# Time mixing in a fused RWKV-6 and expert kernel: the POOL marker gone, queries on DVE, gate results in spare columns of the score banks, the gate over two steps

## The chip, the cores and the metric

The kernel runs on one core of a Trainium2 chip. The metric is the device time of one execution in microseconds (us). A core has a matrix engine (PE, with weight loads shown apart as PEld), a vector engine (DVE), an activation engine (ACT), a general engine (POOL), and SP, which here only issues DMAs. Each engine works through its own queue in order; they meet through semaphores. SBUF is the on-chip memory, PSUM the banks that PE writes.

## What is computed

Two stages. Time mixing (RWKV-6) over 4 batches, 8 heads, 768 positions and head size 48, with a state per head that decays by `w` at each position:

```python
for t in range(S):
    cur = np.einsum('bhd,bhe->bhde', u[None] * kt, vt)
    y[:, :, t] = np.einsum('bhd,bhde->bhe', rt, state + cur)
    state = wt[:, :, :, None] * state + np.einsum('bhd,bhe->bhde', kt, vt)
```

Its result, as 3072 tokens of width 384, goes to a gate of two levels (the best of 4 groups, then the best of that group's 4 experts, each with its softmax weight), and to the one expert chosen: `out = weight * (relu(x @ w1[g, e]) @ w2[g, e])`, with an inner width of 1024.

## The kernel before

**Steps.** Time mixing is cut into 16 steps, `n` = 0 to 15: four batches of `HP` = 4 pairs of heads. One of the pair lies on partitions 0 to 63 and one on 64 to 127. In a step the 768 positions are 12 chunks of 64. The loop `for n in range(TOTAL + 1)` is a software pipeline written by hand for PE, DVE and ACT (`manual_schedule`): their instructions run in the order of the code. POOL and SP are ordered by the planner of the language.

**One step in the order of its code.** `masked(n)`: PE makes two tiles of scores (L311), `q` by `kk` and `ru` by `rk`; DVE masks the first (L318, `at`) and copies the diagonal from the second (L321). `growth(n)`: PE multiplies keys and values (L342), ACT copies the result to `g` (L347). For step n+1, `scaled` makes `ru` and `tot` on ACT (L279, L281), `prefixes` makes the running products `e` on DVE (L287, L289, and the scan L291), `queries` makes `q` = r times e on POOL (L296). `outer(n-1)`: PE adds the contribution of the states to `y` (L387), ACT copies `y` to `xt` (L395). `keys(n+1)` transposes `kk` on PE (L329) with a copy on ACT (L336). `states(n)` is a scan on DVE (L352, `ze`). `suffixes(n+2)` is the scan `s` on DVE (L267) and `kk` = k times s on POOL (L272). `inner(n)`: PE adds the masked scores times the values to `y` (L368), of which there is one buffer. Then loads, `finish(n-1)` and `ordered(n)` (ACT, L362, `zs`).

**The marker.** In `outer`, the half with `cross` set writes to the PSUM bank that matmuls of `inner` of the same step write from other rows of the array. It waits for `mark`, a one-element memset on POOL (L373) that waits for the matmuls of `inner`.

**Gate.** `finish` transposes `xt` into rows of tokens `x` (PE L329, ACT L403) and computes logits on PE (L413) in two banks of their own: 72 matmuls for three pairs of heads when the third of a batch is done, 24 for the last. `gate` runs once a batch, at n = 6, 10, 14 and 16: 19 small DVE operations in a row (L109 to L441), with an exponential on ACT and, in the middle, two matmuls (L428, L429) that count the tokens ahead of each token. Its result `dest` is the slot of every token. `put` sends rows of 128 tokens there with indirect DMAs issued by POOL (L448), six a batch.

**Loads.** SP issues the loads of `w` and `rk` (L159, L164); ACT's queue issues `v` (L168), the weights of the first two experts (L94, L95, at n = 5) and `blanks`, which writes empty slots to the scratch memory (L257, four a step at n = 0 to 3).

**Experts.** After the last `put` the rows are loaded again by expert (`xg`), transposed, multiplied with both weights (L592, L624, L636, L638) and scattered to the output by POOL (L614). The change leaves this part alone.

Of the kernel before, what the change touches and what calls it, by code (L numbers as in the profile page):

```python
# [31 lines left out]
I32 = mybir.dt.int32  # L33
# [15 lines left out]
def rwkv_then_moe(  # L49
# [48 lines left out]
    def choose(pool, lg, n):  # L98
# [14 lines left out]
        nc.scalar.activation(out=low, in_=low, func=AF.Exp)  # L113
# [13 lines left out]
    def weigh(pool, gone, low, sums, n, weight):  # L127
        nc.vector.tensor_reduce(out=sums, in_=low, axis=AX.X, op=ALU.add)
# [10 lines left out]
    with ExitStack() as first:  # L139
# [27 lines left out]
        def load_values(b):  # L167
            nc.scalar.dma_start(out=vts[b % 2][:, 0:VL], in_=v_d[b])  # L168


        nc.vector.memset(ws[0], 1.0)
        nc.gpsimd.memset(rks[0], 0.0)
        load_decays(0)
        load_pair(0)
        first_of = ip.tile([128, WP], F32, name="first_of", tag="first_of")
        nc.vector.memset(first_of, 0.0)
        nc.vector.memset(first_of[:, 0:WP:C + 1], 1.0)
# [4 lines left out]
        gs = [ip.tile([128, D, NB], F32, name=f"g{i}", tag=f"g{i}") for i in range(2)]  # L182
        u_sb = const([128, HP], F32, "u_sb")
        nc.vector.memset(u_sb, 0.0)
        for t in range(2):
            nc.scalar.dma_start(out=u_sb[64 * t:64 * t + D, :], in_=u_d[t])
        for i in range(2):
            nc.vector.memset(ss[i][:, WP:WP + 1], 1.0)
            nc.vector.memset(tots[i][:, :, 0:1], 0.0)
            nc.vector.memset(ivs[i], 0.0)  # L190
        nc.vector.memset(ws[1], 1.0)
        nc.gpsimd.memset(rks[1], 0.0)
        load_decays(1)
# [15 lines left out]
        nc.vector.tensor_scalar(out=si, in0=si, scalar1=C - 1, scalar2=None, op0=ALU.bitwise_and)  # L209
        diag_mask = const([128, C], U8, "diag_mask")  # L210
        nc.vector.tensor_tensor(out=diag_mask, in0=ti, in1=si, op=ALU.is_equal)
        later = const([128, C], F32, "later")
        nc.vector.tensor_tensor(out=later, in0=ti, in1=si, op=ALU.is_gt)

        def numbers(shape, pattern, base, name, mult=0):
            i = const(shape, I32, name + "_i")
            nc.gpsimd.iota(i, pattern=pattern, base=base, channel_multiplier=mult)
            f = const(shape, F32, name)
            nc.vector.tensor_copy(out=f, in_=i)
            return f  # L220
# [10 lines left out]
        wr = const([128, HP, NL], F32, "wr")  # L231
        nc.vector.memset(wr, 0.0)


        seen = const([128, NE], F32, "seen")
        nc.vector.tensor_copy(out=seen, in_=base_of)
        within = const([128, NE, NCH], F32, "within")
        nc.vector.memset(within, 1.0)
        nc.vector.memset(within[:, :, 0:1], 0.0)

        nc.gpsimd.memset(rks[2], 0.0)
        load_pair(2)
        nc.gpsimd.memset(ws[3], 1.0)
        load_decays(3)
        for t in range(2):
            nc.sync.dma_start(
                out=wr[64 * t:64 * t + D],
                in_=wr_d.rearrange("(h t d) n -> t d h n", h=HP, t=2)[t])
        for i in range(2):
            nc.gpsimd.memset(gs[i][:, :, 0:1], 0.0)  # L250
            nc.gpsimd.memset(vts[i][:, VL:], 0.0)
        blank = ip.tile([CAP // 2, 2, RW], F32, name="blank", tag="blank")
        nc.gpsimd.memset(blank, 0.0)
        nc.gpsimd.memset(blank[:, :, DM:DM + 1].bitcast(I32), N)
# [622 lines left out]
```

## Time and profile before

| | us |
|---|---|
| median of 3 runs (lowest to highest) | 580.56 (579.84 to 583.07) |
| the profiled execution | 582.13 |
| its span, first to last instruction | 580.3 |
| time mixing, first scores (step 0) to the first put of the last batch | 15.13 to 243.81 |
| experts, to the end of the span | 257.50 to 580.30 |

A row of the timeline reads: start, duration, engine, line, operation, output <- inputs, shape, count, and in brackets how long the engine had been idle and what released it. "issue" is idle time for which the profile shows no wait. The first scores of step n (L311) stand at 15.13 us (step 0), 24.38 (1), 40.43 (2), 48.52 (3), 65.58 (4), 75.99 (5), 86.26 (6), 100.23 (7), 121.87 (8), 131.83 (9), 142.22 (10), 156.80 (11), 177.12 (12), 187.50 (13), 195.75 (14) and 207.37 (15).

### The profile page before, as it was taken

What the parts mean: (1) busy time and instruction counts of PE and PEld (TensorE: products, weight loads), DVE (VectorE), ACT (ScalarE), POOL (GpSimd) and SP (SyncE); (2) the same over time, 40 slices, a digit from 0 to 9 for tenths busy, and PEclk for the clock granted to TensorE, in tenths of its full rate; (3) what the DMA queues carried; (4) which work ended last, traced back from release to release, by engine and by line L of the source; (5) the groups of instructions that cost most, each with busy time, mean ns of one, the idle gap of its engine ahead of it and who ended that gap; (6) DMA issues with size and microseconds to landing.
All of it is one profiled execution on the core that took longest, in us unless ns stands there. A gap on an engine that the chain in (4) does not pass through costs nothing. (4 is left out here: it accounts for less than half of the span.)

```text
span 580.3 us, 16365 instructions
## 1 busy us (share of the span) xinstructions
PE 468.0 (81%) x7346; PEld 406.9 (70%) x7346; DVE 230.3 (40%) x337; ACT 156.2 (27%) x345; POOL 127.5 (22%) x131
## 2 busy tenths in 40 slices
PE   0656966787477758339999999998999999999990
PEld 0645855587456647338988899888888988898880
DVE  7949389548946941301142455241011101110100
ACT  2445354245435612101211121112111211121110
POOL 7423143523363440120111001010100110001100
PEclk9889698678859955559999999999999999999996
DMA  8997479734242023043555867765646564555000
GB/s 206 252 254 218 138 233 314 263 82 132 60 124 45 5 76 92 14 140 108 190 219 177 259 213 254 231 233 210 243 155 230 172 234 163 215 185 208 16 14 21
DMA packets 20974, 95.77 MB, mean 165 GB/s; under 512 B 4038, under 2 KB 7627, under 8 KB 16288
## 3 DMA queue, kind: packets, MB, share of 16 engines
q1 hardware_dynamic: 14240, 68.63, 38.5%
q10 hardware_dynamic: 3328, 16.55, 8.8%
q0 software_dynamic: 3328, 9.47, 4.4%
q8 instruction: 59, 0.97, 0.7%
q14 instruction: 19, 0.16, 0.1%
HBM read 79.64 MB, written 15.78 MB: 164 GB/s over the span
## 5 line engine op out<-in xcount | busy, mean ns | idle before, releaser
L592 PE MATMUL bank_a<-xt,w 128*128 128x224 f32 x768 | 150.9, 357 | 0.6 <-DVE xt L606 0.6
L592 PEld LDWEIGHTS bank_a<-xt,w 128*128 128x128 f32 x768 | 145.1, 191 | 3.4 <-issue 2.3
L614 POOL DMA_INDIRECT out_dram<-yo,xg x32 | 30.9, 964 | 288.0 <-DVE yo L619 233.2
L624 PE MATMUL bank_b<-w,ht 128*128 128x384 f32 x256 | 85.6, 488 | 0.0
L594 ACT ACTIVATE ht<-bank_a 128x224 f32<-128x224 f32 x128 | 45.7, 357 | 111.4 <-PE bank_a L592 110.0
L619 DVE TENSOR_SCALAR yo<-bank_b,xg 128x384 f32<-128x384 f32 (+1 forms) x32 | 18.1, 566 | 136.7 <-PE bank_b L624 80.6
L624 PEld LDWEIGHTS bank_b<-w,ht 128*128 128x128 f32 x256 | 47.5, 190 | 29.7
L636 PE MATMUL bank_b<-w,ht 128*32 128x288 f32 x768 | 66.8, 409 | 0.0
L638 PE MATMUL bank_b<-w,ht 128*32 128x96 f32 x768 | 66.4, 246 | 0.0
L638 PEld LDWEIGHTS bank_b<-w,ht 128*32 128x32 f32 x768 | 62.9, 110 | 0.0
L606 DVE COPY xt<-bank_b 128x384 f32<-128x384 f32 (+1 forms) x32 | 14.8, 503 | 105.5 <-PE bank_b L604 105.5
L645 ACT COPY yo<-bank_b 32x96 f32<-32x96 f32 x48 | 11.1, 232 | 161.1 <-DVE yo L619 160.8
L636 PEld LDWEIGHTS bank_b<-w,ht 128*32 128x32 f32 x768 | 46.9, 108 | 8.7 <-issue 7.6
L296 POOL TENSOR_TENSOR q<-rk,e 128x768 f32<-128x768 f32 x16 | 37.0, 2312 | 73.1 <-DVE e L291 30.9
L387 PE MATMUL y<-q,zs 64*48 64x64 f32 x704 | 32.5, 251 | 17.7 <-issue 15.7
L267 DVE TENSOR_TENSOR_SCAN s<-w,first_of 128x780 f32<-128x780 f32 x16 | 42.6, 2662 | 1.4 <-DMA w<-in_w_dram 1.4
L387 PEld LDWEIGHTS y<-q,zs 64*48 64x48 f32 x704 | 28.5, 145 | 20.7 <-issue 18.2
L342 PE MATMUL bank<-v,kt 64*64 64x48 f32 x704 | 24.3, 242 | 14.3 <-issue 13.9
L272 POOL TENSOR_TENSOR kk<-rk,s 128x768 f32<-128x768 f32 x16 | 27.3, 1704 | 32.6 <-DVE s L267 14.9
L448 POOL DMA_INDIRECT slot_scratch<-x,dest x24 | 24.4, 1018 | 42.1 <-DVE dest L441 26.0
L342 PEld LDWEIGHTS bank<-v,kt 64*64 64x64 f32 x704 | 20.4, 156 | 16.7 <-issue 16.7
L347 ACT COPY g<-bank 128x288 f32<-128x288 f32 (+1 forms) x32 | 11.6, 420 | 69.0 <-PE bank L342 44.1
(132 smaller groups left out, 516.1 us busy)
## 6 DMA issues: line engine op xcount, KB each, us to landing
w<-in_w_dram SPq DMA_DIRECT2D x28, 1536.0 KB, 6.5
rk<-in_rk_dram SPq DMA_DIRECT2D x32, 288.0 KB, 9.4
w<-in_w_dram ACTq DMA_DIRECT2D x4, 1536.0 KB
slot_scratch<-blank ACTq DMA_DIRECT2D x16, 337.8 KB, 5.8
w<-in_w_dram SPq DMA_DIRECT2D x32, 146.2 KB, 5.5
wt<-in_w_dram SPq DMA_DIRECT2D x4, 1170.0 KB
v<-in_v_dram ACTq DMA_DIRECT2D x4, 1152.0 KB
xg<-slot_scratch SPq DMA_DIRECT2D x16, 193.0 KB
```

Source lines behind the costliest of these rows:

```text
L267: nc.vector.tensor_tensor_scan(out=p["s"][:, 0:WP][:, ::-1], data0=p["w"][:, ::-1], data1=first_of[:, ::-1], initial=1.0, op0=ALU.mult, op ...
L272: nc.gpsimd.tensor_tensor(out=blocked(kk), in0=blocked(p["rk"][:, 1]), op=ALU.mult, in1=p["s"][:, 1:].rearrange("p (n c) -> p n c", c=C + ...
L296: nc.gpsimd.tensor_tensor(out=blocked(p["q"]), in0=blocked(p["rk"][:, 0]), op=ALU.mult, in1=p["e"].rearrange("p (n c) -> p n c", c=C + 1)[ ...
L342: nc.tensor.matmul(zs[j][halves[t], c * D:(c + 1) * D], lhsT=p["kt"][halves[j], c, halves[t]], rhs=value(p, c, t, D)[halves[j]], start=Tru ...
L387: m = nc.tensor.matmul(p["y"][j][64 * t:64 * t + D, C * c:C * (c + 1)], lhsT=p["zs"][halves[t], i], rhs=p["q"][halves[t], C * i:C * (i + 1 ...
L448: m = nc.gpsimd.indirect_dma_start(out=slot_dram, out_offset=bass.IndirectOffsetOnAxis(ap=dest[:, c:c + 1], axis=0), in_=x[:, c, :], in_of ...
L592: nc.tensor.matmul(z[:, 0:n], lhsT=w1[:, dc, f * 128:(f + 1) * 128], rhs=xt[:, dc], start=(dc == 0), stop=(dc == DC - 1))
L594: nc.scalar.activation(out=ht[:, f], in_=z[:, 0:n], func=AF.Relu)
L614: nc.gpsimd.indirect_dma_start(out=out, out_offset=bass.IndirectOffsetOnAxis(ap=to, axis=0), in_=yo[0:m], in_offset=None, bounds_check=N - ...
L624: nc.tensor.matmul(z[0:m, 0:DM], lhsT=ht[:, f, 0:m], rhs=w2[:, f], start=(f == 0), stop=(f == FC - 1))
L636: nc.tensor.matmul(z[32 * g:32 * (g + 1), 0:q], lhsT=lhs, rhs=w2[:, f, 0:q], start=(f == 0), stop=(f == FC - 1), skip_group_check=True)
L638: nc.tensor.matmul(z[96:128, 96 * g:96 * (g + 1)], lhsT=lhs, rhs=w2[:, f, q:], start=(f == 0 and g == 0), stop=(f == FC - 1), skip_group_c ...
```

## The change

- The marker goes. The `cross` half of `outer(n)`, which runs in step n+1, now waits for an instruction that is there anyway and follows `inner(n)`: the last ACT copy of `rows(n-1)` (L418), or, for step 0, the mask multiplication of step 1 (`behind_inner`).
- `queries` moves from POOL to DVE (L305); `q` has three buffers instead of two. POOL keeps `kk` (L279) and the puts.
- Logits and the gate's counts are written to the columns of the second score tile that the scores leave free, instead of banks of their own. So they stand on PE right behind the scores, ahead of `growth`. Logits are split two pairs and two pairs (in the last batch three and one), and their sums over both halves are one DVE reduction (L435).
- The gate is a generator that is resumed at three places: choice and scan after `states` of one step, the two matmuls after the scores of the next, the rest after `queries` of that step. The exponential moves to the start of the last part. Three puts are issued after `kk` of a later step, and three a step later.
- SP joins the hand-written order. All loads, the values and the blanks too, go through SP's queue; blanks at n = 1 to 4, from a tile of half the size that is read twice; weights of expert 0 at n = 5, of expert 1 at n = 7.
- `growth` stands after `ru`, `tot` after `keys`, `rows` right after `inner`; `xt` has three buffers. In the setup, conversions move from DVE to ACT, and part of it behind the first `kk`.

```diff
         def load_values(b):
-            nc.scalar.dma_start(out=vts[b % 2][:, 0:VL], in_=v_d[b])
...
+            nc.sync.dma_start(out=vts[b % 2][:, 0:VL], in_=v_d[b])
+
+        first.enter_context(tc.manual_schedule(engines={
+            ENG.PE, ENG.DVE, ENG.Activation, ENG.SP}))
...
         def queries(p):
-            p["q"] = p2.tile([128, S], F32, name="q", tag="q")
-            nc.gpsimd.tensor_tensor(
+            p["q"] = p2.tile([128, S], F32, name="q", tag="q", bufs=3)
+            nc.vector.tensor_tensor(
...
-            p["behind"] = nc.gpsimd.memset(mark, 0.0)
-            for m in ms:
-                tc.add_manual_dep(p["behind"].ins, m.ins.name, AFTER,
-                                  reason="row tiles share a bank")
...
+        def behind_inner(p, m):
+
+            p["behind"] = m
+            for i in p["inner"]:
+                tc.add_manual_dep(m.ins, i.ins.name, AFTER, reason="row tiles share a bank")
...
+            zs = z.rearrange("p (t x) -> p t x", t=2)[:, :, S // 2:S // 2 + NCH * NL]
...
+        def step(n):
+            p, z, y = (pipe.get(n + i) for i in (0, 1, -1))
+            if n % HP == 0:
+                xs[batch(n)] = vp.tile([128, NCH, RW], F32, name="x", tag="x")
+            spare = masked(p)
+            add = sums(n - 2, spare) if n > 1 else None
+            gating = ready.pop(0) if ready else None
+            if gating:
+                gating.send(spare)
+            if n == 1:
+                behind_inner(y, p["masking"])
+            if z:
+                scaled(z)
+            growth(p)
+            if z:
+                prefixes(z)
+                queries(z)
+            if add:
+                add()
+            if gating:
+                next(gating)
+            if y:
+                outer(y)
+            if z:
+                keys(z)
+                totals(z)
+            states(p)
+            if ready:
+                next(ready[0])
+            if n + 2 < TOTAL:
+                pipe[n + 2] = suffixes(n + 2)
+            inner(p)
+            if y:
+                behind_inner(p, rows(y, xs[batch(n - 1)]))
+            ordered(p)
+            with tc.issue_after(pipe[min(n + 2, TOTAL - 1)]["made"].ins):
+                put(3)
...
+            if 1 <= n <= NE // 4:
+                for e in range(4 * n - 4, 4 * n):
+                    blanks(e)
+            if n in (HP + 1, HP + 3):
+                load_weights((n - HP) // 2)
```

POOL's order around the puts of the first batch, before (steps 5 to 7):

```order
L296 TENSOR_TENSOR q<-rk_88,e 128x768
L272 TENSOR_TENSOR kk<-rk_86,s_100 128x768
L373 MEMSET mark 1x1
L296 TENSOR_TENSOR q<-rk_86,e 128x768
L272 TENSOR_TENSOR kk<-rk_87,s_101 128x768
L373 MEMSET mark 1x1
L296 TENSOR_TENSOR q<-rk_87,e 128x768
L272 TENSOR_TENSOR kk<-rk_88,s_100 128x768
L373 MEMSET mark 1x1
L448 DMA slot_scratch<-x,dest 50688x386 x6
L296 TENSOR_TENSOR q<-rk_88,e 128x768
L272 TENSOR_TENSOR kk<-rk_86,s_101 128x768
```

The same place after the change:

```order
L279 TENSOR_TENSOR kk<-rk_86,s_93 128x768
L279 TENSOR_TENSOR kk<-rk_87,s_94 128x768
L279 TENSOR_TENSOR kk<-rk_88,s_93 128x768
L472 DMA slot_scratch<-x,dest 50688x386 x3
L279 TENSOR_TENSOR kk<-rk_86,s_94 128x768
L472 DMA slot_scratch<-x,dest 50688x386 x3
L279 TENSOR_TENSOR kk<-rk_87,s_93 128x768
```

The multiplications for `q` and the markers have left POOL, and the six puts stand as three and three with a `kk` between.

PE's order at the end of one step and in the next, where logits are due, before (step 7's logits, then step 8):

```order
L329 MATMUL bank<-ident,xt 128x128 x6
L413 MATMUL bank<-wr,xt 64x20 x72
L311 MATMUL scores<-q,kk 64x64 x24
L311 MATMUL scores<-ru,rk_88 64x64 x24
L342 MATMUL bank<-v_89,kt 64x48 x22
L387 MATMUL y<-q,zs 48x64 x22
L329 MATMUL bank<-ident,kk 128x128 x6
```

The same after the change (step 7):

```order
L343 MATMUL bank<-ident,xt 128x128 x6
L320 MATMUL scores<-q,kk 64x64 x24
L320 MATMUL scores<-ru,rk_87 64x64 x24
L431 MATMUL scores<-wr,xt 64x20 x48
L356 MATMUL bank<-v_90,kt 64x48 x22
L402 MATMUL y<-q,zs 48x64 x22
L343 MATMUL bank<-ident,kk 128x128 x6
```

The logits moved from ahead of the scores to behind them, and `growth` (L356) now stands behind the logits.

DVE's order in the step in which the gate's first part runs, after the change (the names from L110 to L122 are those of the choice, L446 is the gate's scan; before, all of these and 11 more stood between the scan `s`, L267, and the next `at`, L318):

```order
L435 TENSOR_REDUCE sum_of<-scores 128x120
L498 TENSOR_TENSOR sum_of<-sum_of 128x120
L366 SCALAR_TENSOR_TENSOR ze<-g_100,tot_98 128x576
L110 TENSOR_REDUCE top<-sum_of 128x30
L112 TENSOR_TENSOR low<-sum_of,top 128x120
L113 TENSOR_TENSOR ones_1287<-sum_of,top 128x120
L115 TENSOR_TENSOR ones_1287<-ones_1287,desc 128x120
L116 TENSOR_REDUCE best<-ones_1287 128x30
L117 TENSOR_TENSOR ones_1287<-desc,best 128x120
L122 TENSOR_TENSOR mine<-ones_1287 128x6x16
L446 SCALAR_TENSOR_TENSOR upto_c<-within,mine 128x96
L274 SCALAR_TENSOR_TENSOR s_94<-w_85,first_of 128x780
```

The gate's first half now stands between `ze` and `s`; its second half follows `q` of the next step.

## Rows read from the trace of the kernel before

**Rows 1.** The page: busy time, share and instructions of each engine.
```profile
PE 468.0 (81%) x7346; PEld 406.9 (70%) x7346; DVE 230.3 (40%) x337; ACT 156.2 (27%) x345; POOL 127.5 (22%) x131
```

**Rows 2.** Table by stretches, its columns in the first line.
```profile
core 0: us, PE busy (x) PEld busy (x) DVE busy (x) ACT busy (x) POOL busy (x), PEclk, DMA share, GB/s
24.40:86.30 61.90, 43.68 (x1416) 39.17 (x1416) 41.18 (x39) 29.90 (x50) 19.16 (x14) 0.83 0.77 216
100.20:121.90 21.70, 17.73 (x383) 15.04 (x384) 9.82 (x14) 4.85 (x9) 10.30 (x9) 0.58 0.59 195
...
187.50:195.75 8.25, 6.36 (x262) 5.60 (x254) 7.40 (x9) 5.05 (x10) 3.85 (x3) 1.00 0.02 4
207.40:243.80 36.40, 23.47 (x485) 20.71 (x484) 9.65 (x31) 5.56 (x11) 5.95 (x7) 0.50 0.23 67
257.50:580.30 322.80, 307.47 (x2652) 265.35 (x2652) 68.93 (x109) 56.84 (x176) 30.86 (x32) 0.98 0.52 178
```

**Rows 3.** Timeline of DVE in step 3.
```profile
50.01 0.93 DVE L318 TENSOR_TENSOR at<-scores,later 128x768 f32<-128x768 f32 x1
51.03 1.04 DVE L321 COPY_PREDICATED at<-diag_mask,scores 128x768 f32<-128x768 uint8 x1
...
52.49 1.78 DVE L291 TENSOR_TENSOR_SCAN e<-w,iv 128x780 f32<-128x780 f32 x1
54.19 1.33 DVE L352 TENSOR_TENSOR_SCAN ze<-g,tot 128x576 f32<-128x576 f32 x1
55.44 1.76 DVE L267 TENSOR_TENSOR_SCAN s<-w,first_of 128x780 f32<-128x780 f32 x1
```

**Rows 4.** Timelines of POOL and of DVE in steps 13 and 14.
```profile
193.12 2.58 POOL L296 TENSOR_TENSOR q<-rk,e 128x768 f32<-128x768 f32 x1 [4.35 <-DVE e L291]
197.47 1.68 POOL L272 TENSOR_TENSOR kk<-rk,s 128x768 f32<-128x768 f32 x1 [1.77 <-PE scores L311]
...
194.14 3.20 DVE L267 TENSOR_TENSOR_SCAN s<-w,first_of 128x780 f32<-128x780 f32 x1
197.26 0.93 DVE L318 TENSOR_TENSOR at<-scores,later 128x768 f32<-128x768 f32 x1
```

**Rows 5.** The last gate on DVE, and waits: us, times, longest.
```profile
238.17 0.28 DVE L109 TENSOR_REDUCE top<-lg 128x30 f32<-128x120 f32 x1
242.73 0.32 DVE L441 TENSOR_REDUCE dest<-upto_c 128x6 int32<-128x96 f32 x1
...
PE bank L428 <- DVE x L431: 14.4, 4, 6.1
```

**Rows 6.** Timelines around the puts of step 11, and a scatter among the experts.
```profile
158.87 1.01 POOL L448 DMA_INDIRECT slot_scratch<-x,dest  x1 [5.17 <-DVE dest L441]
...
165.28 1.33 POOL L448 DMA_INDIRECT slot_scratch<-x,dest  x1 [0.30 <-issue]
...
162.40 0.49 PE L342 MATMUL bank<-v,kt 64*64 64x48 f32 x5 [0.30 <-issue]
...
167.72 0.72 ACT L347 COPY g<-bank 128x288 f32<-128x288 f32 x2 [13.57 <-PE bank L342]
...
275.53 1.00 POOL L614 DMA_INDIRECT out_dram<-yo,xg  x1 [24.39 <-DVE yo L619]
```

**Rows 7.** Timelines of PE and POOL, instruction queue (packets, MB), blanks (KB, us to landing).
```profile
56.09 0.88 PE L387 MATMUL y<-q,zs 64*48 64x64 f32 x12 [3.57 <-issue]
...
37.08 1.68 POOL L272 TENSOR_TENSOR kk<-rk,s 128x768 f32<-128x768 f32 x1 [9.30 <-DMA rk<-in_rk_dram]
...
q8 instruction: 59, 0.97, 0.7%
...
slot_scratch<-blank ACTq DMA_DIRECT2D x16, 337.8 KB, 5.8
```

**Rows 8.** Timelines of PE and of POOL, the two ends of time mixing.
```profile
15.13 1.56 PE L311 MATMUL scores<-q,kk 64*64 64x64 f32 x48
...
243.81 0.97 POOL L448 DMA_INDIRECT slot_scratch<-x,dest  x1 [20.80 <-DVE dest L441]
```

More of the change, by code (lines that the diff above doesn't have):

```diff
@@ L218, in numbers @@
             f = const(shape, F32, name)
-            nc.vector.tensor_copy(out=f, in_=i)
+            nc.scalar.copy(out=f, in_=i)
             return f
@@ L244, in rwkv_then_moe @@
-        load_decays(3)
-        for t in range(2):
-            nc.sync.dma_start(
[L247 to L254, printed above, removed]
@@ L256, in blanks @@
-        def blanks(e):
-            nc.scalar.dma_start(
-                out=slot_dram[e * NR:e * NR + CAP, :].rearrange("(p j) w -> p (j w)", j=2),
-                in_=blank.rearrange("p j w -> p (j w)"))
+        nc.scalar.copy(out=seen, in_=base_of)
+        for i in range(2):
+            nc.vector.memset(ss[i][:, WP:WP + 1], 1.0)
+            nc.vector.memset(tots[i][:, :, 0:1], 0.0)
+            nc.vector.memset(gs[i][:, :, 0:1], 0.0)
+            nc.vector.memset(vts[i][:, VL:], 0.0)
+        nc.vector.tensor_scalar(out=si, in0=si, scalar1=C - 1, scalar2=None, op0=ALU.bitwise_and)
@@ new lines, in rwkv_then_moe, with rest_of_setup @@
+        diag_mask = const([128, C], U8, "diag_mask")
+        nc.vector.tensor_tensor(out=diag_mask, in0=ti, in1=si, op=ALU.is_equal)
+        later = const([128, C], F32, "later")
+        nc.vector.tensor_tensor(out=later, in0=ti, in1=si, op=ALU.is_gt)
+        nc.gpsimd.memset(ws[2], 1.0)
+        load_decays(2)
+        within = const([128, NE, NCH], F32, "within")
+        def rest_of_setup():
+            nc.gpsimd.memset(rks[2], 0.0)
+            load_pair(2)
+            nc.gpsimd.memset(ws[3], 1.0)
+            load_decays(3)
+            nc.gpsimd.memset(ivs[1], 0.0)
+            nc.gpsimd.memset(blank, 0.0)
+            nc.gpsimd.memset(blank[:, DM:DM + 1].bitcast(I32), N)
+            nc.gpsimd.memset(within, 1.0)
+            nc.gpsimd.memset(within[:, :, 0:1], 0.0)
+            nc.gpsimd.memset(ones, 1.0)
@@ L261, in blocked, with blanks @@
+        def blanks(e):
+            nc.sync.dma_start(
+                out=slot_dram[e * NR:e * NR + CAP, :].rearrange("(p j) w -> p j w", j=2),
+                in_=blank[:, None, :].to_broadcast([CAP // 2, 2, RW]))
         def blocked(a):
@@ L402, in rows, with logits @@
             for c0, b in transposed(p["xt"], p["n"]):
-                nc.scalar.copy(
+                m = nc.scalar.copy(
                     out=x[:, c0:c0 + 3, h0:h0 + 2 * D].rearrange("p c (t d) -> p c t d", t=2),
                     in_=b.rearrange("p (c t d) -> p c t d", c=3, t=2)[:, :, :, 0:D])
-        def logits(hps):
-            zs = [bank()[:, 0:NCH * NL].rearrange("p (c n) -> p c n", c=NCH) for _ in range(2)]
+            return m
+        def logits(hps, z):
+            zs = z.rearrange("p (t x) -> p t x", t=2)[:, :, S // 2:S // 2 + NCH * NL]
+            zq = zs.rearrange("p t (c n) -> p t c n", c=NCH)
             for c, j, sl in blocks:
@@ new lines, in sums, with whole @@
+            split = HP - 1 if b == B - 1 else HP // 2
+            if hp == split - 1:
+                part[b], add = logits([(h, xts[h]) for h in range(split)], z)
+                return add
+            if hp == HP - 1:
+                lg, add = logits([(h, xts[h]) for h in range(split, HP)], z)
+                def whole():
+                    add()
+                    nc.vector.tensor_tensor(out=lg, in0=lg, in1=part[b], op=ALU.add)
+                    ready.append(gate(b, lg, xs[b]))
+                return whole
@@ new lines, in rwkv_then_moe @@
+        p = pipe[0] = suffixes(0)
+        scaled(p)
+        prefixes(p)
+        queries(p)
+        with tc.issue_after(p["made"].ins):
+            rest_of_setup()
+        keys(p)
+        totals(p)
+        pipe[1] = suffixes(1)
+        for n in range(TOTAL):
+            step(n)
+        n = TOTAL
+        spare = p_sc.tile([128, 1024], F32, name="scores", tag="scores")
+        sums(n - 2, spare)()
+        outer(pipe[n - 1])
+        spare = p_sc.tile([128, 1024], F32, name="scores", tag="scores")
@@ L528, in rwkv_then_moe @@
+        sums(n - 1, spare)()
+        rows(pipe[n - 1], xs[B - 1])
+        gating = ready.pop(0)
+        next(gating)
+        gating.send(spare)
+        next(gating)
+        put(len(puts))
     mp = ctx.enter_context(tc.tile_pool(name="experts", bufs=2))
```

170 lines of the change are left out of this document (57 added, 113 removed).

## The prediction

> **What bounds the kernel now.** I read the table by stretches first, because the busy shares of the page [rows 1] average two unlike stages. The experts take 322.8 of the span, PE is busy for 307.5 of them at a granted clock of 0.98 [rows 2]: they are bound by PE, and the change leaves them alone. Time mixing ends with the first put of the last batch at 243.81 [rows 8], and only here can time be won. It has no engine that is full. From the first scores at 15.13 [rows 8] to those of step 15 at 207.37 (the list under the table of times), 15 steps take 192.2 us, 12.8 each.
>
> The second view is one step in which nothing but DVE's own work stands in a row: step 3, from `at` at 50.01 to the end of the scan `s` at 57.20, 7.19 us without a gap [rows 3]. The shortest step, 187.50 to 195.75, takes 8.25 at full clock, with PE busy for 6.36, DVE for 7.40 and the DMA share at 0.02 [rows 2]. So a step costs DVE about 7.2 and PE about 6.4 when nothing disturbs it; the rest up to 12.8 is disturbance, and I count four kinds.
>
> First the puts. Step 7, with six, lasts 21.7 [rows 2], and step 11, with six too, 20.3 by the list. While POOL issues them PE gets on with five matmuls in 0.72 us and shows no wait for anything but "issue", and ACT's `g` stands 13.57 for it [rows 6]. Second the gate: its 19 operations from 238.17 to 243.05 are 4.9 us on DVE, and PE waits 14.4 in four for the counts inside it [rows 5]. Third the early loads: in steps 1 to 5, 61.9 us, the DMA share is 0.77 with 216 GB/s [rows 2], POOL waits 9.30 for `rk`, and PE loses up to 3.57 at a boundary where new instructions are fetched [rows 7]. Fourth POOL itself: `q` takes 2.58 there, stands between `e` and the next scores, and while it runs the scan `s` on DVE takes 3.20 [rows 4] against 1.76 alone [rows 3].
>
> **The change part by part**, against the profiled execution (582.1, span 580.3; the median of the runs is 1.6 lower).
>
> *Step without disturbance.* With `q` on DVE the chain e, q, scores, at no longer crosses to POOL. No row shows this multiplication on DVE. The rows nearest to it are the two passes over as many elements, 0.93 and 1.04 [rows 3]; the upper bound is the scan of 780, 1.78 [rows 3]; below nothing lies the case that the 1.44 by which POOL's `q` now holds up `s` were in every step, for then the move gains 0.49. I take 0.95, since it is a plain product like `at`. DVE's floor is then 7.19 + 0.95 = 8.15 a step, and it is the longest: PE's 6.4 lies beneath it at full clock. At half clock PE would be on top: its 485 matmuls in the last stretch, at 0.50, are busy for 48 ns each against 24 in the shortest step [rows 2], up to 12.7 for a step. Which steps run at which clock I leave to the range. 15 steps: 122.3.
>
> *Marker, rows, buffers.* The marker's replacement, the copy of `rows`, follows `inner` within a microsecond or two on PE and ACT, and `outer` of that step comes only after the next scores and `growth`: nothing. Three buffers of `q` let DVE write while `outer` still reads: nothing on DVE's floor. The two banks saved let `growth` and transposes go on: nothing beyond it. `logits` behind the scores wait for DVE's copy of the same bank, since they write into it, and `growth`, `g` and `ze` queue behind them. In that step PE stands until L334 ends; DVE has `e` (1.78) and `q` (0.95) to do meanwhile, which covers 48 short matmuls and most of `growth`; if the cover is gone it costs about 1 us in six steps, within the range.
>
> *Gate.* Split, it gives back PE's waits, but all its operations still lie on DVE, which is now the floor: 4.9 plus two reductions and an addition of 0.28 each, about 5.7 a batch. Three batches before step 15: 17.1.
>
> *Puts.* Three and three, not six; six take from 158.87 to 166.61 [rows 6], 1.3 us each. If PE is held back as now, three cost 3.9, of which a part of the 1.75 between PE's 6.4 and DVE's 8.15 is free; I take 0.65 of it, so 6.5 a batch for the first two. The third batch's have no `kk` left between them and come together, 8. Sum 21. The lower bound is nothing: a scatter among the experts takes as long on POOL [rows 6] while PE runs on.
>
> *Early loads and code.* The bytes don't change, so some waits stay. In before each of steps 1 to 5 loses 12.4 − 8.25 = 4.1 to them and to POOL. I keep about a third, 1.3 a step, 6.5 in all, because weights now come in two parts at steps 5 and 7 and blanks start a step later, so that less stands ahead of `rk`. Fetches of instructions later on: 59 packets [rows 7] over the span, some of whose stalls fall into time mixing after step 5 while loads run: 3 us. [...]
>
> *Start.* `q` at 0.95 instead of 2.58 [rows 4] saves 1.6 ahead of the first scores, and conversions that go from DVE to ACT, by estimate, 0.9: 12.6 instead of 15.1. The bounds are 11 and 15.1.
>
> *End.* From step 15's scores to the first put is 36.4 at clock 0.50 [rows 2]. Six puts of batch 2 stand in it and hold PE up for 8; they now come ahead. `rows` no longer stands ahead of the last logits: 2, an estimate from its six transposes and two copies. So 26.4. The gate's 4.9 in it stays.
>
> *Sum.* Step 15 starts at 12.6 + 122.3 + 17.1 + 21 + 6.5 + 3 = 182.5, the first put of the last batch at 182.5 + 26.4 = 208.9, against 243.8: 34.9 won. The profiled execution would be 582.1 − 34.9 = 547.2, the median 1.6 less, **546**.
>
> **The rivals.**
>
> *The loads keep their price* (22%). Steps 1 to 5 stay at 12.4, since the same megabytes come in the same time at 216 GB/s and one SP queue issues them. Against 8.15 + 1.3 that is 2.95 × 5 = 15 more: 561. For it: the DMA share of 0.77. Against: a part of the 4.1 is POOL's `q` and the marker, and these go.
>
> *Puts and loads are hidden* (13%). If three puts are as harmless as one among the experts [rows 6], and loads come in time, DVE alone counts: 30.5 of the sum (21, 6.5 and 3) go: 515. Against: nothing shows a change in how puts are issued.
>
> *POOL and DVE meet at SBUF* (8%). DVE's scan took 1.44 longer beside POOL's `q` [rows 4]. `kk` on POOL now comes while DVE goes on to products of two SBUF tensors, and each of 16 steps may pay 1.44: 23 more, 569. Against: `kk` ran beside `at` (0.93) unharmed [rows 4], and the order keeps it there. [...]
>
> *Slower: one queue on SP* (8%). SP now works in the written order, and blanks, values and weights stand in it ahead of loads that the next steps need. A blank takes 5.8 to land [rows 7]; if SP waits for earlier transfers so that four of them pass one after the other, a step with blanks takes 23.2 plus about 7 for its loads, 30 against 9.45, in four steps: 82 more, 628. It makes the kernel slower from the point at which steps 1 to 5 take over 9.45 + 34.9 / 5 = 16.4 each. For it: loads are late already (9.30). Against: today's 216 GB/s [rows 2] are only reached by transfers that overlap, many of them from SP's queue.
>
> *The change doesn't act* (3%). POOL is still ordered by the planner, and if `kk` stands behind puts for as long as `q` and the marker did, the chain has only changed its engine: 580.
>
> **How the numbers follow.** 46% for the forecast, with its own range 530 to 560 (`q` at 0.93 to 1.78 is up to 12 more; puts, loads and fetches 15 less; a step or two at half clock 5 to 9 more). The range of 512 to 569 takes in the first three rivals and leaves out about 1 in 10. A measurement of this kernel can tell about 0.5%, 2.9 us: faster 46 + 22 + 13 + 8 = 89%, within it 3%, slower 8%.
>
> **What would show it.** Right: `q` on DVE near 0.95 and no `s` over 2; most steps from 6 on at 8 to 10 us with DVE without gaps; PE's waits for counts gone; "issue" still there beside three puts; step 15's scores near 182. Wrong: steps 1 to 5 at 12 or more with waits for `rk` or `w` (loads); SP standing at blanks with DVE idle behind it (one queue); DVE with gaps while PE is at half clock, which would make PE the floor, 4.5 a step more; `growth` standing behind the logits for over 2 us; a scan of over 3 with `kk` beside it (SBUF).

## The result

The changed kernel takes 563.8 us (median of four runs, 561.46 to 566.1) against 580.2 for the kernel before: a ratio of 0.971, 95% interval 0.966 to 0.977. It is faster, as forecast, but by 16.4 us where 34.9 were expected, and above the forecast's own range of 530 to 560. It is near the 561 of the first rival. The profiled execution of the changed kernel took 561.46, its span 559.4; it lies 20.7 below the profiled one of before (582.13), so the profiles show 4 us more than the medians.

Its page shows where the work went: POOL's busy time falls from 127.5 to 91.9, that of DVE falls too though it has `q` now [rows 1].

```profile
PE 462.1 (83%) x7346; PEld 403.1 (72%) x7346; DVE 224.7 (40%) x346; ACT 156.9 (28%) x348; POOL 91.9 (16%) x100
```

DVE's timeline in step 1 shows why: `q` takes 0.96 and the scan `s` 1.75, as in the step of [rows 3], with no scan beside a `q` on POOL as in [rows 4].

```profile
20.06 0.96 DVE L305 TENSOR_TENSOR q<-rk,e 128x768 f32<-128x768 f32 x1
20.94 1.35 DVE L366 TENSOR_TENSOR_SCAN ze<-g,tot 128x576 f32<-128x576 f32 x1
22.21 1.75 DVE L274 TENSOR_TENSOR_SCAN s<-w,first_of 128x780 f32<-128x780 f32 x1
```

The lengths of the steps, from one step's first scores to the next's, tell where time was won and where not (step 15 up to the first put of the last batch):

| step | 0 | 1 | 2 | 3 | 4 | 5 | 6 | 7 | 8 | 9 | 10 | 11 | 12 | 13 | 14 | 15 |
|---|---|---|---|---|---|---|---|---|---|---|---|---|---|---|---|---|
| before | 9.3 | 16.1 | 8.1 | 17.1 | 10.4 | 10.3 | 14.0 | 21.6 | 10.0 | 10.4 | 14.6 | 20.3 | 10.4 | 8.3 | 11.6 | 36.4 |
| after | 8.1 | 14.3 | 9.2 | 13.7 | 8.2 | 20.8 | 10.3 | 14.3 | 12.2 | 12.6 | 9.4 | 16.2 | 11.3 | 9.7 | 12.9 | 26.9 |

Steps 7 and 11, which had six puts each, and the end give 21; step 10, where PE stood for the gate, 5; step 5 costs 10.5 more than before. The same in the table by stretches, after (steps 1 to 5, step 7, step 15; columns as in [rows 2]):

```profile
core 0: us, PE busy (x) PEld busy (x) DVE busy (x) ACT busy (x) POOL busy (x), PEclk, DMA share, GB/s
21.08:35.36 14.28, 8.37 (x245) 7.37 (x245) 10.72 (x10) 5.86 (x9) 3.37 (x2) 0.76 1.03 283
35.36:44.58 9.22, 6.42 (x246) 5.59 (x245) 6.73 (x8) 5.68 (x11) 0.00 (x0) 1.00 0.67 188
44.58:58.28 13.70, 10.64 (x341) 9.76 (x340) 9.56 (x10) 6.06 (x12) 1.97 (x2) 0.75 0.86 236
58.28:66.49 8.21, 6.48 (x245) 5.66 (x244) 5.71 (x7) 6.13 (x11) 1.40 (x1) 1.00 0.47 103
66.49:87.33 20.84, 11.23 (x342) 10.28 (x341) 11.78 (x20) 5.98 (x11) 1.68 (x1) 0.67 1.01 296
97.60:111.92 14.32, 11.22 (x341) 10.13 (x341) 9.74 (x10) 5.93 (x12) 5.75 (x5) 0.76 0.82 283
196.32:223.25 26.93, 16.49 (x485) 14.45 (x484) 8.79 (x25) 6.98 (x13) 4.83 (x5) 0.78 0.32 90
```

Two kinds of step stand side by side. Steps 2 and 4 run at full clock and take 9.2 and 8.2. Steps 1, 3, 5 and 7 show a granted clock of 0.67 to 0.76, a mix of its two levels, 1.00 and 0.50 (in step 1 it is 1.00 from 21.08 to 27.20 and 0.50 from 27.30 to 34.00); in 1 and 5 the DMA engines are full (1.03 and 1.01). PE's timeline in steps 1 and 5, and the one DVE instruction that waits at the end of the chain:

```profile
29.85 2.15 PE L402 MATMUL y<-q,zs 64*48 64x64 f32 x34 [5.01 <-issue]
...
70.74 0.23 PE L431 MATMUL scores<-wr,xt 64*64 64x20 f32 x1 [2.62 <-DVE iv L296]
72.43 2.68 PE L431 MATMUL scores<-wr,xt 64*64 64x20 f32 x92 [1.46 <-issue]
...
81.64 0.56 PE L356 MATMUL bank<-v,kt 64*64 64x48 f32 x10 [5.53 <-issue]
...
83.16 1.36 DVE L366 TENSOR_TENSOR_SCAN ze<-g,tot 128x576 f32<-128x576 f32 x1 [7.15 <-ACT g L361]
```

PE waits 2.62 for DVE's copy before it may write the logits into the copy's bank (the row names `iv`, L296, the instruction right behind the copy), then 1.46 and 5.53 for nothing but "issue", as at the fetch boundary in [rows 7]; `g` and `ze` come late behind it, and DVE, the engine that was to be the floor, stands for 7.15.

That these "issue" stalls are fetches of instructions can be read from the DMA view, though not from the engines' rows. The queue `q8 instruction` moves packets of 0.02 MB. All ten stalls at "issue" of 0.9 us or more in steps 1 to 14 end 1.3 to 1.7 us after the end of such a packet. In step 1 PE stops at 24.83; the packet begins only at 27.31, takes 1.02, and PE goes on at 29.85. In step 5 PE stops at 76.11, the packet begins at 78.76 and takes 1.33, and PE goes on at 81.64. So half of each long stall passes before the packet begins. The stall of 3.57 in [rows 7], from 52.52 to 56.09, has such a packet too, between 53.7 and 54.7 (`q8 instruction: 1, 0.02, 5.8%` of that stretch). Queues (packets, MB, share of the DMA engines) from 24.8 to 27.3, where other transfers take all of it, and from 24.8 to 29.9:

```profile
q1 hardware_dynamic: 106, 0.93, 99.2%
...
q8 instruction: 1, 0.02, 1.2%
```

The waits over time mixing (us, times, longest):

```profile
PE scores L320 <- issue: 15.6, 21, 2.1
PE scores L431 <- DVE iv L296: 11.4, 6, 3.4
PE scores L451 <- DVE iv L296: 6.5, 3, 2.6
SPq L165 <- PE scores L320: 68.0, 10, 19.2
```

Of the 14.4 that PE waited inside the gate [rows 5] one wait of 2.6 is left, in step 15, but 18 us before logits and counts took their place. Loads are not late: only at the start do `kk` and `ru` wait for `rk` (3.6 at most, up to 16.2 us), and it is SP that waits 68 us until a tile may be overwritten. So the first rival's figure nearly came true, and not by late data.

### The profile page after: what moved, and what is told of

The parts are those of the page before. It is cut to its first block, busy times and chain, and to the rows that moved or that the text cites. A ratio compares the mean times of both kernels' runs of the same rounds, so it can differ in the third digit from the quotient of the medians.

```text
span 559.4 us, 16323 instructions
## 1 busy us (share of the span) xinstructions
PE 462.1 (83%) x7346; PEld 403.1 (72%) x7346; DVE 224.7 (40%) x346; ACT 156.9 (28%) x348; POOL 91.9 (16%) x100
## 5 line engine op out<-in xcount | busy, mean ns | idle before, releaser
L279 POOL TENSOR_TENSOR kk<-rk,s 128x768 f32<-128x768 f32 x16 | 27.8, 1737 | 135.3 <-DVE s L274 77.0
L402 PE MATMUL y<-q,zs 64*48 64x64 f32 x704 | 34.9, 271 | 6.7 <-issue 6.7
L402 PEld LDWEIGHTS y<-q,zs 64*48 64x48 f32 x704 | 32.7, 164 | 7.0 <-issue 7.0
L431 PE MATMUL scores<-wr,xt 64*64 64x20 f32 x768 | 21.0, 242 | 15.9 <-DVE iv L296 11.4
L431 PEld LDWEIGHTS scores<-wr,xt 64*64 64x64 f32 x768 | 19.1, 175 | 17.7 <-DVE iv L296 12.3
L361 ACT COPY g<-bank 128x288 f32<-128x288 f32 (+1 forms) x32 | 11.6, 419 | 72.0 <-PE bank L356 72.0
L472 POOL DMA_INDIRECT slot_scratch<-x,dest x24 | 25.0, 1043 | 33.7 <-issue 26.4
L300 DVE TENSOR_TENSOR_SCAN e<-w,iv 128x780 f32<-128x780 f32 x16 | 28.5, 1783 | 0.6
L274 DVE TENSOR_TENSOR_SCAN s<-w,first_of 128x780 f32<-128x780 f32 x16 | 28.1, 1758 | 0.0
```

What stands on the lines that cost most here:

```text
L274: nc.vector.tensor_tensor_scan(out=p["s"][:, 0:WP][:, ::-1], data0=p["w"][:, ::-1], data1=first_of[:, ::-1], initial=1.0, op0=ALU.mult, op ...
L279: p["made"] = nc.gpsimd.tensor_tensor(out=blocked(kk), in0=blocked(p["rk"][:, 1]), op=ALU.mult, in1=p["s"][:, 1:].rearrange("p (n c) -> p ...
L300: nc.vector.tensor_tensor_scan(out=p["e"], data0=p["w"], data1=p["iv"], initial=0.0, op0=ALU.mult, op1=ALU.add)
L402: m = nc.tensor.matmul(p["y"][j][64 * t:64 * t + D, C * c:C * (c + 1)], lhsT=p["zs"][halves[t], i], rhs=p["q"][halves[t], C * i:C * (i + 1 ...
L431: nc.tensor.matmul(zq[halves[j], t, c], lhsT=xt[hs, sl], rhs=wr[hs, hp], start=(hp == hps[0][0]), stop=(hp == hps[-1][0]), skip_group_chec ...
L472: m = nc.gpsimd.indirect_dma_start(out=slot_dram, out_offset=bass.IndirectOffsetOnAxis(ap=dest[:, c:c + 1], axis=0), in_=x[:, c, :], in_of ...
```

## The experiments

Three theories were set against each other. **F**: PE runs out of instructions, since their fetch takes longer while transfers are in flight. **L**, later **C**: logits and counts wait for DVE's copy, and the clock falls behind the wait. **P**: the puts. Later letters are told where they come. Each kernel is the changed kernel with the edit named, and with one more copy of a mask in a path that these inputs don't take. The runs come from several chips: on some the kernel before takes 579 to 581, on others 560. Times are compared within a chip and ratios across chips, with care, since the two kinds differ in what a put costs (last section).

**The changed kernel beside the edits** (e0_control, e0_again, e0_third).

> The changed kernel again, beside the three edits of the same chip, with one copy of a mask more in the path for rare inputs, which these inputs don't take. Every theory: 562 to 566 us, ratio to the kernel before about 0.971, the stalls of PE at the same places (5.0 us at 24.3 to 29.9, 5.5 at 76 to 81.6).

> The changed kernel once more, as the measure for the three others of this chip (the chips of the first two groups of runs differ: the kernel before took 578.7 on one, 560.1 on the other, and on the second PE ran on beside the puts). All theories: 0.965 to 0.975 of the kernel before.

> The changed kernel, as the measure for the three others of this chip: 0.965 to 0.975 of the kernel before.

563.3, 563.6 and 563.8 us, ratios 0.969, 0.973, 0.973. These are the measures for the runs beside them.

**Weights late** (e1_late_weights):

```diff
-            if n in (HP + 1, HP + 3):
-                load_weights((n - HP) // 2)
+            if n in (TOTAL - 3, TOTAL - 2):
+                load_weights(n - TOTAL + 3)
```

> The weights of experts 0 and 1 are loaded at steps 13 and 14 instead of 5 and 7; nothing else moves. Theory F (PE runs out of instructions, because their fetch queues behind the transfers in flight): step 5 falls from 20.8 us to 12 to 14, its stall of 5.5 goes, step 7 loses 1 to 2; one or two stalls of 2 to 5 appear in steps 13 to 15, where transfers are now. Sum 554 to 559. Theory L (logits and counts that stand behind DVE's copy and ahead of growth are what ate the gain): step 5 stays above 18, sum 562 to 565. Theory P (the puts): 562 to 565.

564.9 against 563.3: nothing. The stall of step 5 stands without any weights in flight. The weights now come in step 13 (second row, columns as in the table by stretches):

```profile
78.97 0.56 PE L356 MATMUL bank<-v,kt 64*64 64x48 f32 x10 [5.06 <-issue]
...
169.91:184.30 14.39, 10.68 (x341) 9.76 (x341) 12.07 (x19) 6.27 (x12) 1.68 (x1) 0.76 0.95 397
```

So F was wrong on what is in the way in step 5. And nearly full DMA engines (0.95, 397 GB/s) cost stalls of only 0.9 and 0.8 in step 13 (the first right behind a wait of 2.0 for the copy, which may cover a part of it).

**Logits behind growth, then behind outer** (e2_logits_behind_growth, e7_logits_behind_outer, e7_again). The second moves the same three lines behind `outer(y)`:

```diff
-            add = sums(n - 2, spare) if n > 1 else None
-            gating = ready.pop(0) if ready else None
-            if gating:
-                gating.send(spare)
...
             growth(p)
+            add = sums(n - 2, spare) if n > 1 else None
+            gating = ready.pop(0) if ready else None
+            if gating:
+                gating.send(spare)
```

> On PE the logits and the counts of the gate stand behind growth instead of ahead of it, in the same spare columns. Theory L: PE's waits for DVE's copy (L431 and L451, 18 us in 9) are hidden by growth, steps 3, 5, 7, 9, 11 and 13 lose 1 to 2 each, sum 552 to 557. Theory F: the fetch stalls stay, at most the waits of ze for g (1.5 to 1.7 in three steps) go, sum 559 to 563. Theory P: 559 to 564.

> On PE the logits and counts stand behind growth and outer, so that DVE's copy is done before they begin. Theory C: PE's waits of 1 to 3.5 us for the copy go, the clock stays at full in steps 7, 9, 11 and 13, each of which loses 2 to 4: sum 550 to 556. Theory F: 560 to 564, since the stalls of the fetches stay and drop the clock as before.

> Logits and counts behind outer, beside the changed kernel on one chip. Theory C: 6 to 12 us less than the changed kernel. Theory F: 0 to 4 less: in the steps with fetch stalls the wait for DVE's copy only takes the place of a stall.

Behind growth: 561.6 against 563.3, within the scatter; PE still waits 2.4 to 2.6 for the copy in steps 11 and 13, where growth doesn't cover it. Behind outer: 556.4 against 563.6 on one chip, 7.2 less, ratio 0.958 (0.950 to 0.966); on another chip 541.3 beside a kernel before of 560.1 (0.973). PE's waits from 66 to 177 us, about steps 5 to 12, changed kernel (e0_again) and e7_again:

```profile
PE bank L356 <- issue: 8.3, 11, 4.2
PE scores L431 <- DVE iv L296: 7.2, 4, 2.6
PE scores L320 <- issue: 6.3, 3, 4.0
PE scores L451 <- DVE iv L296: 3.4, 2, 1.9
PE scores L431 <- issue: 2.8, 5, 1.2
```

```profile
PE scores L431 <- DVE iv L296: 0.5, 1, 0.5
PE scores L431 <- issue: 8.3, 9, 4.0
PE scores L320 <- issue: 8.2, 9, 4.0
PE bank L356 <- issue: 7.4, 7, 4.6
```

The waits for the copy are gone, 7.2 us are won, and theory C has the size right. But in these steps nothing is won: all stalls at "issue" together grow from 18.2 to 28.2, and from the first scores of step 5 to those of step 13 the two kernels take 105.2 and 107.8. That was theory F's reason: where fetches stall, a wait for the copy only takes the place of a stall. The first put of the last batch comes 7.1 earlier; 5.0 of it lie before step 5, where the runs of the changed kernel themselves differ by 3.4, 2.7 in steps 13 and 14, where hardly a transfer is under way (DMA share 0.02 and 0.01 in the changed kernel), and 2.1 in step 15; steps 5 to 12 take 2.6 back.

**No puts** (e3_no_puts): `put(3)` in the steps becomes `puts.clear()`.

> Leaves out the 18 puts of batches 0 to 2 (their tokens get no result), so that POOL issues indirect DMAs only after the last gate. Theory P: steps 7, 8, 11, 12 and the 8 us of stop and go at the scores of step 15 all go, 15 to 18 us, sum 546 to 549. Theories F and L: the puts cover other waits in part, steps 7 and 11 stay at 11 to 12 because of their logits or fetches, sum 551 to 556.

545.9 against 563.3: 17.5 less, theory P's figure. But most of it falls in step 15, which takes 18.5 up to the first put, at a clock of 0.93, where e0_control on the same chip takes 31.7 at 0.62. Step 15 in both, without puts first:

```profile
189.95:208.47 18.52, 11.69 (x485) 10.67 (x484) 8.64 (x25) 6.85 (x13) 0.00 (x1) 0.93 0.30 67
...
194.78:226.45 31.67, 21.19 (x485) 18.86 (x484) 10.09 (x27) 7.16 (x14) 6.17 (x6) 0.62 0.27 77
```

Steps 1 to 5 are nearly as long as with puts (63.7 against 65.7). The puts were priced about rightly (21); the missing time is elsewhere.

**q on POOL** (e4_q_on_pool, e4_again): `nc.vector` becomes `nc.gpsimd` in `queries`.

> The changed kernel with q = r times e back on POOL, all else as changed. If the move of q is what brings most of the gain (its step in the prediction): 1.4 for s and about 1.6 for the chain e, q, scores in each of 15 steps come back in part, sum 574 to 582. If the rest of the change (puts, gate, order of rows) carries it, and the fetches and the half clock set the steps: 564 to 570.

> The changed kernel with q on POOL, beside the changed kernel on one chip. If moving q is what brings most of the gain: 10 to 16 us more than the changed kernel. If the fetches set the early steps and puts, gate and tail carry the gain: 2 to 7 more (first group of numbers: first put of the last batch at 210 with q on POOL, 205 and 204 in two variants with q on DVE).

566.1 against 563.6: 2.5, within the scatter and not 10 or more. `s` takes 2.35 in the mean again (1.76 with `q` on DVE), and hardly anything comes of it, probably because DVE has the time where PE is late anyway: in e4_again it waits 24.1 us for PE's scores ahead of L330 and L334. On the other chip q on POOL took 550.0 beside 560.1 (0.985), without a changed kernel to compare.

**Half of the blanks** (e6_half_blanks): `out` is only the rows from `CAP // 2` on.

> Writes blank rows only to the upper half of each expert's slots (these inputs fill the lower half with tokens), 2.7 MB instead of 5.4 in steps 1 to 4; nothing else moves. Theory F (instruction fetches take long while transfers are in flight): the 5 us stalls of steps 1 and 5 fall to 2 to 4, sum 557 to 561. Theory C (it is the wait for DVE's copy in the steps with logits, and the half clock behind it): 562 to 565.

543.5 beside a kernel before of 560.1 (0.974); no changed kernel ran on that chip, so this can't be weighed. The stall of step 5 is 3.2, that of step 1 4.7.

**No loads** (e10_no_loads):

> Leaves out the loads of w and rk for steps 4 to 15 and of v for batches 2 and 3 (the steps compute with old tiles), and loads the weights of experts 0 and 1 at steps 13 and 14; blanks and puts stay. Its tokens go to other experts, so only the time up to the first put of the last batch counts, 223 to 226 in the changed kernel. Theory F: with nothing in flight between steps 6 and 12 no stall at an instruction boundary is left there (10 us of them without puts), and those of steps 1 to 5 shrink with the traffic: first put at 203 to 212. Theory C: the stalls fall but steps with logits stay at 12 to 14: 215 to 221. If stalls of 2 to 4 stay where no transfer is in flight, F is wrong.

The first put of the last batch stands at 196.0 (no changed kernel ran on that chip; with q on POOL it stood at 210.1). In steps 4 to 14 PE's stalls at fetches are nearly gone (66 to 177 us, columns as above), but the waits for the copy stay:

```profile
PE scores L431 <- DVE iv L296: 9.2, 4, 2.6
...
PE scores L320 <- issue: 1.1, 2, 0.9
```

Steps 5 to 12 take 82.0, against 97.2 in e6_half_blanks on the same chip. This bears F out: from 73.5 to 177.4 us the DMA share is 0.08, and no stall at "issue" there is longer than 0.52. In steps 1 to 3, where 16 blanks now follow each other closely, stalls of 3.1, 5.8 and 2.5 stay. The one of 5.8, in step 2, with the DMA view from its start to the beginning of the fetch's packet (40.5 to 43.3):

```profile
46.28 0.98 PE L402 MATMUL y<-q,zs 64*48 64x64 f32 x14 [5.77 <-issue]
...
DMA packets 432, 0.62 MB, mean 222 GB/s; under 512 B 30, under 2 KB 432, under 8 KB 432
...
q1 hardware_dynamic: 432, 0.62, 108.5%
```

The DMA engines are full and all 432 packets are under 2 KB. So rows don't have to be long for a stall of this size.

**More traffic of short rows** (e12_more_traffic): four writes of [112, 2, 384] from `blank` to scratch memory in each of steps 9, 10 and 11.

> Twelve more writes of 344 KB, of the shape of the blanks, to scratch memory that nothing reads, four in each of steps 9, 10 and 11, where little else is in flight. No engine but SP waits for them. Theory F (the fetch of PE's instructions takes longer while transfers are in flight): stalls of 1.5 to 5 at instruction boundaries appear in steps 9 to 12, where they had 2.0 to 2.5 in all, and these steps grow by 6 to 12 together. Theory D (transfers cost time only through late data): no engine waits longer, at most 1 us more.

563.9 against 563.6: nothing. One stall came up:

```profile
150.97 0.71 PE L343 MATMUL bank<-ident,xt 128*128 128x128 f32 x5 [2.04 <-issue]
```

Steps 9 to 11 take 40.3 against 40.5, with a DMA share of 0.72, 0.70 and 0.63 where e0_again has 0.49, 0.42 and 0.37. F as first put is wrong: more bytes in flight alone don't do it.

**Where v comes in** (e13_values_in_thirds, e15_no_values, e14_outer_thirds_late). Theory V: it is the load of v that holds the fetch. Theory B: any bytes alike.

> The load of v for the next batch (1152 KB) is cut into three of 384 KB, issued in the first three steps of a batch instead of all in the first; nothing else moves. Theory V (the fetch that PE lacks waits behind v's transfer in the same engines: the stalls of 4 to 5.5 fall into steps 1, 5 and 9, each right behind an issue of v): these three stalls shrink to 1 to 2.5, one or two of 1 to 2 may appear in steps 2, 3, 6, 7, 10 and 11; sum 5 to 9 less than the changed kernel. Theory B (any bytes in flight count alike): the stalls move from the first steps of a batch to the others, 0 to 3 less.

> Leaves out the loads of v for batches 1 to 3 (they use the values of batch 0; tokens may go to other experts, so the first put of the last batch counts, 224 in the changed kernel). Theory V: the stalls of steps 1, 5 and 9 fall to under 1.5, and with them the half clock behind them: first put 8 to 14 earlier. Theory B: 3.5 MB less of about 25 in these steps is a seventh of the stalls, 2 to 4 earlier.

> Three edits in one: logits and counts behind outer, v in thirds, weights of experts 0 and 1 at steps 13 and 14. Theory V: 12 to 16 less than the changed kernel. Theory B: 7 to 9 less, that of the first edit alone.

Thirds: 562.8 against 563.8, nothing. Without v: the stalls of steps 1, 5 and 9 are 2.1, 1.2 and 1.0 instead of 5.8, 6.6 and 1.7, and the first put stands 6.7 earlier: between V and B. All three edits in one: 553.5, ratio 0.951 (0.945 to 0.958), 10.3 less than the changed kernel. That is 3 more than logits behind outer alone had given on another chip, not clear of the scatter.

**Long rows against short ones** (e16_values_again, e17_outer_short_rows). Theory R: what holds the fetch is transfers with long rows (9216 bytes in v, 6144 in rk), not bytes.

```diff
-            if n % HP == 0 and batch(n) + 1 < B:
+            if n % HP == 0 and batch(n) + 1 < B or n in (9, 10, 11):
                 load_values(batch(n) + 1)
```

> The changed kernel, with the load of v for batch 3 (1152 KB, rows of 9216 bytes) issued at steps 8, 9, 10 and 11 instead of at step 8 alone; the data are the same. It is the sister of e12 with long rows for short. Theory R (what holds the fetch of PE's instructions is long rows in flight): stalls of 2 to 5 in steps 10, 11 and 12, each of which had under 1 (step 12 some 2, beside the puts), and 5 to 12 more in these steps. Theory B (any bytes alike): as e12, where 1.4 MB more a step cost one stall of 2.0 and nothing in time.

555.8 us beside a kernel before of 560.0 (0.993). Each added v is followed by a stall, of 1.5, 2.1 (where e12 had its 2.0) and 5.0; the one issued in step 11 has this (SP's issue, then PE):

```profile
156.12 0.38 SPq L169 DMA_DIRECT2D v<-in_v_dram  x1
...
163.94 1.30 PE L402 MATMUL y<-q,zs 64*48 64x64 f32 x20 [5.02 <-issue]
```

Steps 9 to 11 take 46.6, where e6_half_blanks, on a chip of the same kind and as the changed kernel in these steps, takes 38.6. The DMA share in them is 0.57 to 0.64, less than in e12. But e12 differs in more than its rows: it writes in pieces of 344 KB, and a v is read in one piece of 1152 KB. Then the reverse, rk and v cut into rows of 1536 bytes, with logits behind outer:

```diff
+                for i in range(2):
+                    for k in (0, S // 2):
+                        nc.sync.dma_start(out=rks[n % NRK][64 * t:64 * t + D, i, k:k + S // 2],
+                                          in_=rk_d[n // HP, n % HP, t][:, i, k:k + S // 2])
...
+            m = S // 2 if b else VL
+            for k in range(0, VL, m):
+                nc.sync.dma_start(out=vts[b % 2][:, k:k + m], in_=v_d[b][:, k:k + m])
```

> Logits and counts behind outer, and from step 0 on the loads of rk and v are cut into pieces with rows of 1536 bytes (eight DMAs for an rk instead of two, six for a v instead of one); the first loads stay whole. Theory R: the stalls of steps 1, 3, 5 and 9 shrink to under 2, 4 to 10 less than with the first edit alone (0.958 of the kernel before), unless SP, with 0.4 us for an issue, becomes late. Theory B: the same stalls, 0.955 to 0.965.

529.8 us beside a kernel before of 560.0: ratio 0.948 (0.940 to 0.955), the fastest of all. With logits behind outer alone the ratio had been 0.973 (0.963 to 0.983), beside a kernel before of the same time on another chip. Steps 1 to 5 in one stretch, of e7_logits_behind_outer and of e17, then steps 1 and 5 of e17:

```profile
23.41:86.34 62.93, 41.39 (x1422) 37.30 (x1417) 41.44 (x49) 30.34 (x50) 8.41 (x5) 0.86 0.89 240
...
23.16:73.30 50.14, 39.59 (x1423) 35.70 (x1417) 41.46 (x50) 29.93 (x50) 8.44 (x5) 0.88 0.76 206
...
23.20:31.60 8.40, 7.18 (x252) 6.32 (x244) 6.98 (x8) 5.45 (x9) 1.69 (x1) 0.89 0.76 183
...
60.50:73.30 12.80, 9.36 (x342) 8.54 (x341) 10.15 (x17) 6.28 (x11) 1.69 (x1) 0.87 0.75 215
```

Against e7_logits_behind_outer step 1 falls from 12.6 to 8.4, step 5 from 20.1 to 12.8, and the stalls at "issue" of steps 1 to 5 from 21.0 to 10.1. The bytes of the whole are the same, but not those of these steps: by the rows 10.3 MB move in them instead of 15.1. Eight pieces in place of two make SP issue for longer (4.55 to 8.30 us for those of an `rk`, where the changed kernel's two take 0.78 to 2.70), and blanks, of which SP issues the first at 37.41 instead of 24.82 in the changed kernel, and weights come later. So three things changed at once: the length of a row, the transfers queued at a time, and the bytes in these steps.

Theory R as put, that it is long rows, doesn't hold by itself: e10 has a stall of 5.8 with nothing but short rows under way, and e1 stalls of 0.9 and 0.8 beside rows of 12288 bytes. That the stalls come with transfers in flight is shown, by e10 in steps 4 to 14 (2.1 us at "issue" from 66 to 177 us, where e6_half_blanks, on the same chip, has 15.8) and by the place of the fetch's packet in the stall (it begins 2.5 and 2.7 us after PE stops, in steps 1 and 5). Which property of theirs brings them stays open; e13, with v in rows of 3072 bytes, doesn't tell either.

## Why the prediction was wrong

The terms, by the timelines of the profiled execution:

| | forecast | measured |
|---|---|---|
| first scores | 12.6 | 13.0 |
| steps 0 to 5 (8.15, five of 9.45, 3 for logits and half a gate) | 58.4 | 74.3 |
| steps 6 to 14 (the rest, with 21 for puts) | 111.5 | 109.0 |
| step 15 to the first put | 26.4 | 26.9 |
| first put | 208.9 | 223.25 |

- **The step that failed** is the term on early loads and code. It kept "about a third" of what steps 1 to 5 lost, 6.5 us, because less would stand ahead of `rk`. The 61.9 of [rows 2] became 66.2 instead, 16 more than forecast, and this is more than the 14.4 by which the first put is late. Two things were wrong in it. What is lost isn't time in which data are late but time in which PE has no instructions: its stalls at "issue" in these steps were 11 us before and are 19 after. The row with 3.57 was read [rows 7] and booked as a small rest, though it stood in the stretch with a DMA share of 0.77. The prediction weighed what was ahead of a load in its queue, not what was ahead of an instruction fetch. And the transfers of this stretch didn't shrink: 61.9 us at 216 GB/s [rows 2] are 13.4 MB, 66.25 at 242 are 16.0:

```profile
21.08:87.33 66.25, 43.14 (x1413) 38.66 (x1413) 44.51 (x53) 29.70 (x49) 8.42 (x5) 0.79 0.87 242
```

  In e17 steps 1 to 5 take 50.1, just about the 50.25 of the forecast, but with logits moved too and fewer bytes in them, so the agreement is in part luck.
- **The second failing** is the logits. Their wait for DVE's copy was seen and put at "about 1 us in six steps, within the range". PE waits 18 us in nine steps. In some of these steps the clock falls too, though not in each; that the wait brings it about was not shown. In step 14 the clock falls to its lower level inside a wait of 2.4 (1.00 from 183.43 to 187.60, 0.50 from 187.80 to 194.40), and PE is busy for 10.07 with 249 matmuls. In step 10 it stays at the higher level (1.00) in spite of a wait of 2.6, and PE is busy for 6.77 with 250. The lower clock of step 3 began behind a fetch stall of 1.8 that ended at 47.32 (1.00 from 34.20 to 47.70, 0.50 from 47.80 to 54.50). Steps 10 and 14:

```profile
136.74:146.18 9.44, 6.77 (x250) 6.05 (x249) 8.96 (x21) 6.05 (x13) 1.67 (x1) 1.00 0.42 99
...
183.43:196.32 12.89, 10.07 (x249) 9.03 (x248) 10.86 (x22) 6.41 (x12) 3.02 (x3) 0.74 0.01 3
```

  Moving the logits behind outer is worth 7.2, none of it in steps 5 to 12.
- **DVE's floor was sized rightly.** `q` takes 0.96, and from one copy to the next DVE runs all of a step's operations without a gap in 8.04, against 8.15:

```profile
61.63 1.02 DVE L334 COPY_PREDICATED at<-diag_mask,scores 128x768 f32<-128x768 uint8 x1 [1.39 <-PE scores L320]
...
69.67 1.01 DVE L334 COPY_PREDICATED at<-diag_mask,scores 128x768 f32<-128x768 uint8 x1
```

  But it bounds few steps. The 8.21 of step 4 are near it by chance, for DVE is busy for 5.71 of them. So moving `q` was worth 2.5 at most.
- **The puts held** in size, 17.5 against 21, but the third batch's fall into step 15, not ahead of it. So the end of 26.4, worked out without them, was too long by some 8: without puts it is 18.5. The two errors hide each other in the sum. On the chips where PE runs on beside puts (last section), the price of 21 would probably have been too high.
- **Start and gate held.** 13.0; the gate's halves take 2.5 and 2.3, and PE's waits for counts became waits for the copy, but for the 2.6 in step 15.
- **The rivals.** The first (561) had about the right price and half the reason: the early steps stay as long as they were, but through PE's instructions. The one queue on SP didn't come: SP waits for PE. The meeting of POOL and DVE came once, at the start, where `q` beside the first `kk` took 2.25:

```profile
8.90 2.57 POOL L279 TENSOR_TENSOR kk<-rk,s 128x768 f32<-128x768 f32 x1 [3.56 <-DMA rk<-in_rk_dram]
...
10.03 2.25 DVE L305 TENSOR_TENSOR q<-rk,e 128x768 f32<-128x768 f32 x1
```

  The other fifteen `q` take 0.96 and the other `kk` 1.67 to 1.69, and no scan `s` takes over 1.77. Why the two take longer side by side was not shown.

## What to carry to other kernels

Where PE runs through short matmuls, look first at its stalls at "issue" in stretches with full DMA engines, and at the packets of the instruction queue: here such stalls took 19 us in five steps, and with the loads left out (e10) 2.1 us of them were left from 66 to 177 us, where e6_half_blanks, on the same chip, has 15.8. Try smaller pieces, or fewer transfers in those steps, before moving work between engines. Results put into a bank that DVE still read made PE wait for DVE here, 18 us in nine steps, and in step 14 the clock was at 0.50 from that wait on; place such writes where the reader is surely done, and expect little of it where PE would stall anyway: of the 7.2 us it won here, none came in steps 5 to 12. When a term is dropped because "less stands ahead", name the queue it stands in, and add up the bytes of that stretch.

## What was not expected of the hardware

Puts don't always hold PE up. In the runs beside a kernel before of 578.7 to 580.9, PE gets on with five or six matmuls in 0.75 us while POOL issues a put, as in [rows 6]; here after, in step 12:

```profile
163.06 1.01 POOL L472 DMA_INDIRECT slot_scratch<-x,dest  x1 [0.16 <-ACT x L418]
...
165.12 0.36 PE L320 MATMUL scores<-ru,rk 64*64 64x64 f32 x6 [0.40 <-issue]
```

In those beside a kernel before of 560 it runs on; e7_logits_behind_outer, step 8:

```profile
114.06 0.97 POOL L472 DMA_INDIRECT slot_scratch<-x,dest  x1 [0.30 <-issue]
...
114.09 1.43 PE L402 MATMUL y<-q,zs 64*48 64x64 f32 x44
```

Counted over the 18 puts of the first three batches, PE starts 10 to 17 matmuls per us of put in the runs of the first kind and 26 to 38 in those of the second. The chips were different ones, and 20 us lie between them for the same kernel. Why is open.
